# Strided values in two pieces, late constants, bf16 maxima and one tile width: a change to an attention and mixture-of-experts kernel

## The chip, the cores and the metric

The kernel runs on one NeuronCore of a Trainium2 chip. It has five engines with an instruction stream each: TensorE (matrix products into the accumulator memory PSUM), VectorE, ScalarE, GpSimd and SyncE, which here only starts transfers. Sixteen DMA engines move data between HBM and the on-chip memory SBUF; transfers are started by SyncE (most), ScalarE (five constants at the start) and GpSimd. The metric is the device time of one execution in microseconds, the median of several runs.

## What is computed

A batch of 8 sequences of 576 tokens passes 8 attention heads of width 64. The first four heads are local (a query sees itself and the 31 keys before it), the last four strided (a query sees the keys before it at distances that are multiples of 32). Then 4,608 tokens of width 512 are assigned to 8 experts, each with a capacity of 576 tokens, in the order of the gate's logits, and every expert is a two-layer network.

```python
scores = scale * np.matmul(q, k.transpose(0, 1, 3, 2))
rel = pos[:, None] - pos[None, :]
mask_local = (rel >= 0) & (rel < stride)
mask_strided = (rel >= 0) & (pos[None, :] % stride == pos[:, None] % stride)
...
attn = np.exp(scores - np.max(scores, axis=-1, keepdims=True))
attn = attn / (np.sum(attn, axis=-1, keepdims=True) + 1e-09)
x = np.matmul(attn, v)          # then [tokens, heads * 64]
...
logits = x @ w_gate             # greedy, largest logit first, capacity N // E
h = np.maximum(x[mask] @ w1[e], 0.0)
out[mask] = h @ w2[e]
```

## The kernel before, in words

Attention is worked off in 16 units (class `Unit`, list `todo`): for each of the 8 batches first the four strided heads, then the four local ones. A unit has two halves `p`, each a pair of heads, so there are 32 half-units, and the loop over `i` (the steps) runs from -1 to 31. It is an order written out by hand: in step `i` the scores of half-unit `i + 1` are finished (`close_scores`), its maxima taken, half-unit `i` is multiplied with the values (`mix`) and normalised (`norm`), the scores of half-unit `i + 2` are begun (`open_scores`), and then the maxima of `i + 1` are subtracted and the exponential is taken (`shift`). Dictionaries of small jobs (`fills`, `drips`, `mids`, `late`) are worked off at given steps: the f16 copy of the attention output (`finish`), its store to a scratch tensor in HBM (`store`), the transposed reload (`turn`), gate logits, scales.

The strided heads are stored sorted by residue, so that a strided head becomes a block-diagonal one: 32 residues of 18 positions. A half of the sequence (288 positions) is cut into 6 groups: five of 54 positions (3 residues, `SQ`) and a last one of 18 (`SLAST`, 288 - 5 x 54). The two sequence halves sit on partitions 0 to 63 and 64 to 127. In `dots` (L341 to 350) a group's scores are four matmuls with the keys as the stationary operand; in `mix` (L382 to 394) a group's output is, for each head of the pair, two matmuls with the exponentials `pr` as the stationary operand and the values `vn` (4 heads by 65 columns, the 65th a one for the sum) as the moving one. For the last group both use 18 columns of the array (`u.wide`, L277), for the others 54. The local heads use groups of 32 queries and 64 keys.

The maxima (`max_main` L352, `max_t` L356): VectorE reduces the scores by blocks of 32 with a transpose, TensorE spreads the result, VectorE reduces it again into `mr` (L362), and L364 to L367 make of it a pair of bf16 numbers (rounded value and remainder) and a diagonal matrix `dd`, with which TensorE subtracts the maxima from the scores in PSUM (L372). ScalarE takes the exponential from there (L376).

Loads are issued by SyncE in the program's order (`load` L305, `load_v` L315): the values of a unit as two transfers, one for each sequence half (54 partitions for a strided unit, 32 for a local one), then keys and queries as one each. Unit `k` is loaded at the start of step `2 (k - 3)`, units 0 to 3 ahead of the loop. The values live in two buffers for each kind, so the load waits until the unit two batches earlier has been mixed. SyncE also issues the reload of transposed outputs (L446), about half of the strided stores (L436; GpSimd issues the rest) and the local stores (L440, L441). Its waits hold up whatever stands behind them. Transfers of SyncE and ScalarE use a ring of eight semaphores: each issue waits until the transfer eight before it has landed.

Ahead of the loop, behind the loads of units 0 to 3, `late_constants` (L164, called in L572) loads seven tables that routing uses: `desc_h`, `fold`, `small`, `tri`, `pick`, `iota`, `val`. The first of them to be read is `desc8h`, in jobs from step 24 on (`PEAKS`).

After attention come routing (searches for the threshold of each expert) and the expert networks, in which weights are loaded, split into f16 parts and multiplied. The change does not touch that code.

Of the kernel before, what the change touches and what calls it, by code (L numbers as in the profile page):

```python
# [8 lines left out]
F32 = mybir.dt.float32  # L9
# [3 lines left out]
AF = mybir.ActivationFunctionType  # L13
OP = mybir.AluOpType
# [4 lines left out]
B, H, S, D = 8, 8, 576, 64  # L19
# [4 lines left out]
HS = S // 2  # L24
LT, LQ, LK = 9, 32, 64
ST, SR = 6, 3
SQ = SR * NA
SLAST = HS - (ST - 1) * SQ
NB = S // 32
BANK = 512  # L30
OPEN_S, OPEN_L = 1, 3
MAX_FIRST = True
WARM = {(-2, 0): 11, (-1, 0): 3, (-1, 2): 3, (31, 0): 2}
B_LATE, L_AT, G5, GW_AT = 5, 8, 6, 4
# [98 lines left out]
def band_stride_attention_then_capacity_moe(ctx, tc, qt, kl, ks, nl, ns, wg, w1, w2, cst, out, dbg=None):  # L133
# [30 lines left out]
    def late_constants():  # L164
        for t, name in ((desc8h, "desc_h"), (fold, "fold"), (small, "small"), (tri, "tri"), (pick, "pick"), (iota, "iota")):
            split_of = {"iota": NC, "pick": 2 * NT}.get(name)
            nc.sync.dma_start(t, cst[name].rearrange("q (s c) -> q s c", c=split_of) if split_of else cst[name])
        nc.sync.dma_start(val[:, :2], cst["val"].rearrange("q (a c) -> q a c", a=2))
# [51 lines left out]
    with tc.tile_pool(name="ld", bufs=2) as ld, \  # L220
# [12 lines left out]
        nc.scalar.activation(warm_e, ones_f[:, :1], AF.Exp)  # L233
        po_all = ps_o.tile([128, 2, BANK], F32, name="po")
        nc.vector.memset(po_all, 0.0)
        for g in "sl":
            for i in range(2):
                t = ld.tile([128, 32], F32, name=f"mx_{g}{i}", bufs=1)
                nc.gpsimd.memset(t, 0.0)
                mxb[g, i] = t  # L240
                t = ld.tile([128, ST if g == "s" else LT, 4, VW], F32, name=f"v_{g}{i}", bufs=1)
                nc.gpsimd.memset(t[:, 0] if g == "l" else t, 0.0)
                vbuf[g, i] = t
# [21 lines left out]
        class Unit:  # L265
# [39 lines left out]
            def load(u, parts=(slice(0, 2),), v=True):  # L305
                b, g = u.b, u.g
                if v:
                    u.load_v()
                u.kt = ld.tile([128, 2, u.nk], F32, name="k" + g)
                u.q = ld.tile([128, 2, S], F32, name="q" + g)  # L310
                for p in parts:
                    nc.sync.dma_start(u.kt[:, p], (ks if u.strided else kl)[b, :, p])
                    nc.sync.dma_start(u.q[:, p], qt[b, :, u.p0 + p.start:u.p0 + p.stop])

            def load_v(u):  # L315
                u.vn = vbuf[u.g, u.b % 2]
                for f in range(2):
                    r = slice(64 * f, 64 * f + SQ) if u.strided else slice(64 * f + 32, 64 * f + 64)
                    nc.sync.dma_start(u.vn[r], (ns if u.strided else nl)[u.b, f])

            def copy_v(u, k):
                vn, n = u.vn, LT // 3
# [18 lines left out]
            def dots(u, p, ts_):  # L341
                for t in ts_:
                    n = u.wide(t)
                    o = u.nq * t
                    for f, h in ((0, 0), (1, 1), (0, 1), (1, 0)):
                        c = HS * f + SQ * t if u.strided else LQ * (2 * t + f)
                        m = n if u.strided else LK
                        r = slice(64 * h, 64 * h + 64)
                        nc.tensor.matmul(u.sp[p][64 * f:64 * f + m, h, o:o + n], u.kt[r, p, c:c + m], u.q[r, p, c:c + n],
                                         start=False, stop=False, skip_group_check=True)  # L350

            def max_main(u, p):  # L352
# [3 lines left out]
            def max_t(u, p):  # L356
                pm = u.sp[p][:, 1, HS:HS + 64]
                for k in range(4):
                    nc.tensor.matmul(pm[32 * k:32 * k + 32], mxb[u.g, p], ident[:, 64 * (k % 2):64 * (k % 2) + 64],
                                     start=False, stop=False, skip_group_check=True)  # L360
                mr = wk.tile([128, 32], F32, name="mr")
                nc.vector.tensor_reduce(mr, pm.rearrange("r (g c) -> r c g", c=32), axis=AX.X, op=OP.max)  # L362
                mh = wk.tile([128, 32], BF16, name="mh")
                nc.vector.tensor_copy(mh, mr)  # L364
                nc.vector.tensor_tensor(mh[64:], mr[64:], mh[64:], op=OP.subtract)
                u.dd = wk.tile([128, NB, 32], BF16, name="dd")
                nc.vector.tensor_tensor(u.dd, mh[:, None, :].to_broadcast([128, NB, 32]), bm, op=OP.mult)  # L367

            def shift(u, p):
                df = u.dd.rearrange("r n c -> r (n c)")  # L370
                for h in range(2):
                    nc.tensor.matmul(u.sp[p][:, h, :HS], sel, df[:, HS * h:HS * h + HS], start=False, stop=True,  # L372
                                     skip_group_check=True)
                pr = wk.tile([128, S], F32, name="pr")
                u.pr[p] = pr
                nc.scalar.activation(pr.rearrange("k (h n) -> k h n", h=2), u.sp[p][:, :, :HS], AF.Exp, scale=0.125)  # L376

            def slots(u, ts_):
                a, b = (0, u.nt) if ts_ is None else (ts_[0], ts_[-1] + 1)
# [2 lines left out]
            def mix(u, p, h, ts_=None, po=None):  # L382
                j0, j1 = u.slots(ts_)
                n = j1 - j0
                po = po_all[:, h, :n * VW] if po is None else po[:, h * n * VW:(h + 1) * n * VW]
                po = po.rearrange("q (t d) -> q t d", d=VW)
                pr = u.pr[p]
                for t in range(u.nt) if ts_ is None else ts_:
                    n, o = u.wide(t), u.place(t, h)
                    for f in range(2):  # L390
                        j, r = (t, 64 * f) if u.strided else (t // 2, 64 * (t % 2) + 32 * f)
                        k = slice(64 * f, 64 * f + 64)
                        nc.tensor.matmul(po[r:r + n, j - j0], pr[k, o:o + n], u.vn[k, t, 2 * p + h],  # L393
                                         start=(j == j0), stop=(j == j1 - 1), skip_group_check=True)

            def norm(u, p, ts_=None, po=None):
# [172 lines left out]
            u.load_v()  # L569
        for u in todo[2:4]:  # L570
            u.load(v=False)
        late_constants()  # L572
        last = 2 * nu - 1
        edge = (B - 2) * S // TP

# [29 lines left out]
        for i in range(-1, 2 * nu):  # L605
            u, n, m = pair(i), pair(i + 1), pair(i + 2)
            if i > 0 and i % 2 == 0 and i // 2 + 3 < nu:
                todo[i // 2 + 3].load()
            if n:
                close_scores(n)  # L610
            warm(i, 0)
            for f in drips.get(i, []):
                f()
            if m or i in mids:
                a = room(m) if m else ps_a.tile([128, 2, 512], F32, name="spa")
            if i in mids or i in mids2 or i in mids3:
                b = ps_b.tile([128, 512], F32, name="spb")
            if u:
                if u[1] == 0:
                    u[0].begin()  # L620
                if i < last:
                    u[0].mix(u[1], 0)
            if i < last:
                for f in mids.get(i, []):
                    f(a, b)
            if i == last:
                gate_scale(B - 1)
                warm(i, 1)
                pt = ps_a.tile([128, 2, 512], F32, name="spa")
                pt = pt[:, 0], pt[:, 1]  # L630
                p1 = ps_b.tile([128, 512], F32, name="spb")
                for ts_, p_ in zip(parts, (None, p1)):
                    for h in range(2):
                        u[0].mix(u[1], h, ts_, p_)
                    u[0].norm(u[1], ts_, p_)
                break
            if n and MAX_FIRST:
                n[0].max_t(n[1])
            if u:
                u[0].mix(u[1], 1)  # L640
            if n and not MAX_FIRST:
                n[0].max_t(n[1])
            if i == last - 1:
                gates(B - 2, ps_a.tile([128, 2, 512], F32, name="spa"))
            warm(i, 1)
            if m:
                open_scores(m)
            warm(i, 2)
            if u:
                u[0].norm(u[1])  # L650
            if i in mids2:
                mids2[i].total_v(b)
            if i == 1:
                todo[1].scale_v()
            for f in mids3.get(i, []):
                f(a, b)
            if i == -1:
                todo[0].square_v()
            if n:
                n[0].shift(n[1])  # L660
            warm(i, 3)
            if i in (-1, 0):
                todo[1].square_v(i + 1)
            if i == 0:
                nc.scalar.activation(jkw, wg_sb, AF.Square, accum_out=sqw)
            for f in late.get(i, []) + fills.get(i, []):
                f()
# [659 lines left out]
```

## Time and profile before

| what | value |
|---|---|
| median of 3 runs (lowest, highest) | 732.16 us (729.22, 738.2) |
| the profiled execution | 732.86 us, of it the span of its instructions 731.1 us |
| attention, about | 0 to 236 us |
| routing and experts | 236 to 731 us |
| TensorE clock granted, mean of the span | 0.871 |
| moved by the DMA engines | 111.23 MB in 106,873 packets |

The page of a profile lists busy times of engines, the DMA queues, groups of equal instructions and their waits. Further views answer from the same trace: a table of busy times by stretch (columns: length, then busy us and, in brackets, instructions of PE, PEld, DVE, ACT and POOL, then granted TensorE clock, mean busy share of the 16 DMA engines and GB/s), a timeline (start, length, engine, line, operation, output<-inputs, shape, count and, in square brackets, idle time before it with what ended it), waits (engine, line, what it waited for: us in total, times, longest) and the DMA queues of a stretch (packets, MB, share of the engines' time). PE is the matmul side of TensorE and PEld its weight loads; DVE is VectorE, ACT ScalarE, POOL GpSimd, SPq SyncE's queue. `L349` is line 349 of the kernel. "issue" as a releaser says that the profile shows nothing that the engine waited for.

### The profile page before, as it was taken

Reading aid. Unit: us, or ns where it says so; the run is one execution under the profiler, and the core shown is the slowest. Engines: PE = TensorE matmul, PEld = TensorE weight load, DVE = VectorE, ACT = ScalarE, POOL = GpSimd, SP = SyncE. Lnnn points to the kernel's source line nnn. Section 1 sums busy time; section 2 is a strip of 40 time slices with the busy share of each in tenths; the row PEclk is TensorE's granted clock in tenths of the full one; section 3 lists DMA queues with packets and bytes.
Section 4 is the critical chain, followed back from the end, with each engine's and each line's share of the span. In section 5 each row is a group of like instructions: output and inputs, shape, how many; then the busy total and the mean of one; then the engine's idle time right before and its main releaser. Section 6 shows DMA issues by size and latency. Waiting matters only on the chain.

```text
span 731.1 us, 19141 instructions
## 1 busy us (share of the span) xinstructions
PE 622.4 (85%) x8043; PEld 410.6 (56%) x8043; DVE 456.3 (62%) x1368; ACT 320.2 (44%) x497; POOL 154.1 (21%) x152
## 2 busy tenths in 40 slices
PE   6878886875889348999999997998998997999993
PEld 3656664654667326645845743754754753665741
DVE  3686666754787777887677674776766763652200
ACT  3444334435252024757166273356347345853210
POOL 2043223133133011032032032015005014212011
PEclk8575657878696557999999998999999999999998
DMA  9989999799764145076076087067068069561010
GB/s 217 247 244 251 215 237 202 210 238 173 212 133 97 36 159 160 1 281 146 1 281 144 1 288 139 1 229 183 16 218 207 1 222 254 211 114 51 1 37 29
DMA packets 106873, 111.23 MB, mean 152 GB/s; under 512 B 75644, under 2 KB 83414, under 8 KB 106275
## 3 DMA queue, kind: packets, MB, share of 16 engines
q1 hardware_dynamic: 98707, 88.46, 47.4%
q0 software_dynamic: 7360, 21.15, 9.5%
q8 instruction: 63, 1.03, 0.6%
q10 hardware_dynamic: 720, 0.39, 0.2%
q14 instruction: 23, 0.19, 0.1%
HBM read 73.60 MB, written 18.87 MB: 126 GB/s over the span
## 4 chain that ended last, share of the span: by engine, by line
PE 21%; DMA 14%; issue 13%; DVE 8%; SPq 4%; ACT 2%; POOL 2%; POOLq 0%; ACTq 0%; DVEq 0%
PE ph L1155 16%; DMA w<-in_w_dram 8%; DMA xg<-x_scr,idx 3%; SPq L1071 3%; PE ph L1203 3%; DMA xt<-xg 2%; DVE w2l L1017 2%; SPq L983 1%; POOL out_dram L1214 1%; ACT jk L998 1%; DVE hl L1163 1%; POOL xg L1068 1%; DVE cm L774 1%; ACT yl L1210 0%; DVE y L1211 0%
## 5 line engine op out<-in xcount | busy, mean ns | idle before, releaser
L1155 PE MATMUL ph<-xt,w1h 128*128 128x288 f16 (+2 forms) x1024 | 179.8, 291 | 13.0 <-DMA xt<-xg 9.4
L1155 PEld LDWEIGHTS <-w1h 128*128 128x128 f16 x1024 | 98.6, 99 | 44.2 <-issue 9.2
L1214 POOL DMA_INDIRECT out_dram<-y,idx x40 | 43.6, 1091 | 342.2 <-ACT y L1213 314.4
L1155 PE MATMUL ph<-xt,w1l 128*128 128x288 f16 (+2 forms) x512 | 113.9, 292 | 0.0
L998 ACT ACTIVATE jk<-w 128x1024 f16<-128x1024 f32 x64 | 67.5, 1054 | 75.1 <-DMA w<-in_w_dram 73.2
L1203 PE MATMUL ph<-w2h,hh 128*128 128x512 f16 x256 | 97.0, 379 | 0.0
L1203 PE MATMUL ph<-w2h,hl 128*128 128x512 f16 x256 | 97.0, 379 | 0.0
L1203 PE MATMUL ph<-w2l,hh 128*128 128x512 f16 x256 | 97.0, 379 | 0.0
L1162 ACT ACTIVATE hh<-ph 128x576 f16<-128x576 f32 (+2 forms) x72 | 42.9, 596 | 120.3 <-PE ph L1155 117.6
L1203 PEld LDWEIGHTS <-hh 128*128 128x128 f16 x512 | 48.4, 98 | 59.6 <-issue 9.7
L1163 DVE SCALAR_TENSOR_TENSOR hl<-ph,hh 128x576 f16<-128x576 f32 (+2 forms) x72 | 49.5, 688 | 42.2 <-ACT hh L1162 41.9
L376 ACT ACTIVATE pr<-spa 128x576 f32<-128x576 f32 x32 | 20.8, 650 | 110.3 <-PE spa L372 92.9
L1155 PEld LDWEIGHTS <-w1l 128*128 128x128 f16 x512 | 50.6, 100 | 13.8 <-issue 0.8
L424 POOL TENSOR_TENSOR xos<-xs,xos 118x768 f16<-118x768 f32 x16 | 26.7, 1672 | 122.8 <-ACT xos L423 122.8
L1068 POOL DMA_INDIRECT xg<-x_scr,idx x40 | 41.6, 1039 | 49.0 <-issue 34.7
L1017 DVE SCALAR_TENSOR_TENSOR w1l<-w,w_sw,w1h 128x512 f16<-128x512 f32 x64 | 45.8, 747 | 9.1 <-ACT w1h L1016 3.9
L1017 DVE SCALAR_TENSOR_TENSOR w2l<-w,w_sw,w2h 128x512 f16<-128x512 f32 x64 | 45.8, 745 | 7.9 <-ACT w2h L1016 7.8
L393 PE MATMUL po<-v_s,pr 64*54 64x65 f32 (+1 forms) x768 | 42.7, 268 | 7.2 <-issue 4.7
L1213 ACT ACTIVATE y<-ph,so 128x512 f32<-128x512 f32 x32 | 21.9, 683 | 57.4 <-PE ph L1203 37.8
L1016 ACT ACTIVATE w1h<-w,w_sw 128x512 f16<-128x512 f32 x64 | 41.7, 709 | 3.2 <-DVE ss_e L203 1.8
L1016 ACT ACTIVATE w2h<-w,w_sw 128x512 f16<-128x512 f32 x64 | 41.1, 710 | 3.7 <-DVE w_sw L208 3.6
L1203 PEld LDWEIGHTS <-hl 128*128 128x128 f16 x256 | 25.0, 98 | 29.4 <-issue 3.6
(613 smaller groups left out, 972.6 us busy)
## 6 DMA issues: line engine op xcount, KB each, us to landing
w<-in_w_dram SPq DMA_DIRECT2D x64, 512.0 KB
v_s<-in_ns_dram SPq DMA_DIRECT2D x16, 329.1 KB
kl<-in_kl_dram SPq DMA_DIRECT2D x8, 608.0 KB
v_l<-in_nl_dram SPq DMA_DIRECT2D x16, 292.5 KB
ql<-in_qt_dram SPq DMA_DIRECT2D x8, 576.0 KB
x_scr<-xol SPq DMA_DIRECT2D x8, 512.0 KB
ks<-in_ks_dram SPq DMA_DIRECT2D x7, 576.0 KB
qs<-in_qt_dram SPq DMA_DIRECT2D x7, 576.0 KB
```

Of the source, the lines that this page charges most:

```text
L393: nc.tensor.matmul(po[r:r + n, j - j0], pr[k, o:o + n], u.vn[k, t, 2 * p + h], start=(j == j0), stop=(j == j1 - 1), skip_group_check=True)
L424: eng.tensor_tensor(u.xo[:nr, :, 1, c], xf, u.xo[:nr, :, 0, c], op=OP.subtract)
L998: nc.scalar.activation(jk, wf[:, c * n4:(c + 1) * n4].rearrange("p c f -> p (c f)"), AF.Square, scale=1.41422, accum_out=sq[:, c:c + 1])
L1016: nc.scalar.activation(hi[:, c, f], wf[:, c, f], AF.Copy, scale=s_)
L1017: nc.vector.scalar_tensor_tensor(lo[:, c, f], wf[:, c, f], s_, hi[:, c, f], op0=OP.mult, op1=OP.subtract)
L1068: nc.gpsimd.indirect_dma_start(out=xg[:n], out_offset=None, in_=x_rows, in_offset=bass.IndirectOffsetOnAxis(ap=idx[:n, t:t + 1], axis=0))
L1071: nc.sync.dma_start_transpose(xt[:, :, t * 128:t * 128 + n], xg[:n])
L1155: nc.tensor.matmul(tile_[:, j, :w], wt[:, d, f * 128:(f + 1) * 128], xt[:, d // 2, xx, d % 2, c], start=(k == 0), stop=(k == 3 * DC - 1))
L1162: nc.scalar.activation(hv, src, AF.Relu)
L1163: nc.vector.scalar_tensor_tensor(lv, src, 0.0, hv, op0=OP.max, op1=OP.subtract)
L1203: nc.tensor.matmul(py, a[:, f, ts_], w[:, f], start=(k == 0), stop=(k == len(todo) - 1))
L1214: st = nc.gpsimd.indirect_dma_start(out=out_rows, out_offset=bass.IndirectOffsetOnAxis(ap=idx[:n, t:t + 1], axis=0), in_=y[:n], in_offset= ...
```

## The change

- The values of a strided unit are loaded as four transfers in place of two: for each sequence half 48 rows and then 6.
- `late_constants` is called in step 13 of the loop, ahead of that step's other work and after the loads of step 12, in place of ahead of the loop.
- `mh`, the maxima rounded to bf16, is written by a VectorE operation with two operands (the maximum of `mr` with itself) in place of a copy.
- The last strided group uses 54 columns of the array like the others, in `dots` and in `mix`. For that the stationary operands are read past their end: strided keys and exponentials move into fixed buffers (`ktb`, `prb`) with 36 further columns, which GpSimd fills at the start with zeros and ones. The further rows of the scores are masked, the further rows of the output are not stored. In the first key half the read reaches into the second key half's columns. The number of matmuls is the same.

```diff
@@ constants, set-up
+CONST_AT = 13
...
+        ktb = [ld.tile([128, 2 * S + SQ - SLAST], F32, name=f"ks{i}", bufs=1) for i in range(2)]
+        prb = [wk.tile([128, S + SQ - SLAST], F32, name=f"pr{i}", bufs=1) for i in range(2)]
+        for i in range(2):
+            nc.gpsimd.memset(ktb[i][:, 2 * S:], 0.0)
+            nc.gpsimd.memset(prb[i][:, S:], 1.0)
@@ load
-                u.kt = ld.tile([128, 2, u.nk], F32, name="k" + g)
+                u.kt = ktb[b % 2] if u.strided else ld.tile([128, 2 * u.nk], F32, name="kl")
...
-                    nc.sync.dma_start(u.kt[:, p], (ks if u.strided else kl)[b, :, p])
+                    nc.sync.dma_start(u.kt[:, p.start * u.nk:p.stop * u.nk].rearrange("q (p n) -> q p n", n=u.nk),
+                                      (ks if u.strided else kl)[b, :, p])
@@ load_v
                 for f in range(2):
-                    r = slice(64 * f, 64 * f + SQ) if u.strided else slice(64 * f + 32, 64 * f + 64)
-                    nc.sync.dma_start(u.vn[r], (ns if u.strided else nl)[u.b, f])
+                    for i, n in ((0, 48), (48, SQ - 48)) if u.strided else ((0, 32),):
+                        r = 64 * f + (i if u.strided else 32)
+                        nc.sync.dma_start(u.vn[r:r + n], (ns if u.strided else nl)[u.b, f, i:i + n])
@@ dots
-                        m = n if u.strided else LK
+                        m = SQ if u.strided else LK
...
-                        nc.tensor.matmul(u.sp[p][64 * f:64 * f + m, h, o:o + n], u.kt[r, p, c:c + m], u.q[r, p, c:c + n],
+                        nc.tensor.matmul(u.sp[p][64 * f:64 * f + m, h, o:o + n], u.kt[r, p * u.nk + c:p * u.nk + c + m], u.q[r, p, c:c + n],
@@ max_t
-                nc.vector.tensor_copy(mh, mr)
+                nc.vector.tensor_tensor(mh, mr, mr, op=OP.max)
@@ shift
-                pr = wk.tile([128, S], F32, name="pr")
-                u.pr[p] = pr
+                pr = u.pr[p] = prb[p]
...
@@ mix
-                    n, o = u.wide(t), u.place(t, h)
+                    o = u.place(t, h)
...
-                        nc.tensor.matmul(po[r:r + n, j - j0], pr[k, o:o + n], u.vn[k, t, 2 * p + h],
+                        nc.tensor.matmul(po[r:r + u.nq, j - j0], pr[k, o:o + u.nq], u.vn[k, t, 2 * p + h],
@@ order of the work
             u.load(v=False)
-        late_constants()
...
                 todo[i // 2 + 3].load()
+            if i == CONST_AT:
+                late_constants()
```

More of the change, by code (lines that the diff above doesn't have):

```diff
@@ L373, in shift @@
                                      skip_group_check=True)
-                pr = wk.tile([128, S], F32, name="pr")
-                u.pr[p] = pr
-                nc.scalar.activation(pr.rearrange("k (h n) -> k h n", h=2), u.sp[p][:, :, :HS], AF.Exp, scale=0.125)
+                pr = u.pr[p] = prb[p]
+                nc.scalar.activation(pr[:, :S].rearrange("k (h n) -> k h n", h=2), u.sp[p][:, :, :HS], AF.Exp, scale=0.125)
             def slots(u, ts_):
```

## The prediction

> **What bounds the kernel now.** I read the page first (slices, queues), then the table by stretches of time, the waits, the timeline of the longest gap, SyncE's timeline and the DMA view around that gap.
>
> ```profile
> PE 622.4 (85%) x8043; PEld 410.6 (56%) x8043; DVE 456.3 (62%) x1368; ACT 320.2 (44%) x497; POOL 154.1 (21%) x152
> ...
> q8 instruction: 63, 1.03, 0.6%
> ...
> 0.00:236.00 236.00, 186.31 (x4453) 134.53 (x4453) 155.19 (x419) 98.32 (x125) 66.97 (x69) 0.75 0.87 205
> ```
>
> The change touches attention alone, 0 to 236 us, where the DMA engines are 87% busy (second number from the right) and TensorE was granted 0.75 of its clock. Routing and experts start when the last logits exist, so what attention gains should reach the end one to one.
>
> ```profile
> SPq L319 <- PE po L393: 23.1, 7, 5.2
> ...
> 124.82 1.17 PE L349 MATMUL spa<-qs,ks 64*54 64x54 f32 x36 [5.70 <-issue]
> 183.97 0.26 PE L349 MATMUL spa<-qs,ks 64*18 64x18 f32 x6 [6.41 <-issue]
> ...
> 97.02:124.82 27.80, 19.99 (x510) 14.88 (x509) 17.95 (x46) 13.10 (x18) 9.30 (x8) 0.75 0.96 225
> ...
> q1 hardware_dynamic: 1208, 1.78, 105.4%
> ...
> q8 instruction: 1, 0.02, 5.4%
> ```
>
> TensorE's long gaps are put down to "issue": no semaphore that the profile knows ended them. From the end of the gap at 97.02 (row further below) to that at 124.82 lie 510 + 509 matmuls and weight loads, 1,024 with a few instructions of the sequencer. Queue q8 says why such a round number: 1.03 MB over 2 x 8043 instructions is 64 B each, so each of its 63 packets of 16 KB holds 256, and four packets 1,024. TensorE waits for its own instructions. The last two rows are the DMA view of 114.4 to 122.2 us (no q8 packet among 1,208 of q1) and of 122.2 to 123.4 (one q8 packet); TensorE resumes at 124.82. So that fetch went through only when a burst of loads had passed. Here is the burst on SyncE:
>
> ```profile
> 84.39 0.72 SPq L319 DMA_DIRECT2D v_s<-in_ns_dram  x2
> ...
> 86.11 8.66 SPq L446 DMA_TRANSPOSE xtl<-x_scr  x1
> ...
> 99.72 0.80 SPq L319 DMA_DIRECT2D v_l<-in_nl_dram  x2
> ...
> 101.70 6.58 SPq L446 DMA_TRANSPOSE xts<-x_scr  x1
> ...
> 111.67 1.18 SPq L319 DMA_DIRECT2D v_s<-in_ns_dram  x2
> 113.83 8.98 SPq L446 DMA_TRANSPOSE xtl<-x_scr  x1
> ...
> 113.00:114.60 1.60, 0.85 (x38) 0.61 (x37) 1.48 (x5) 0.36 (x1) 0.00 (x0) 1.00 0.51 168
> 118.50:119.50 1.00, 0.62 (x5) 0.29 (x4) 0.88 (x4) 0.34 (x1) 1.00 (x1) 1.00 0.91 304
> ...
> v_s<-in_ns_dram SPq DMA_DIRECT2D x16, 329.1 KB
> kl<-in_kl_dram SPq DMA_DIRECT2D x8, 608.0 KB
> v_l<-in_nl_dram SPq DMA_DIRECT2D x16, 292.5 KB
> ql<-in_qt_dram SPq DMA_DIRECT2D x8, 576.0 KB
> ks<-in_ks_dram SPq DMA_DIRECT2D x7, 576.0 KB
> ```
>
> A transpose's issue ends when the loads before it are through. The strided burst (values twice 329.1 KB, keys and queries 576 each, 1,810 KB) takes 94.77 - 84.39 = 10.4 us and 122.81 - 111.67 = 11.1; the local burst (1,769 KB) 108.28 - 99.72 = 8.6. The stretch 113.0 to 114.6, when only the 54-row values move, has 0.51 of the DMA engines busy at 168 GB/s; with keys and queries, 0.91 at 304. So 54 rows use about 9 of 16 engines. The loop is thus: SyncE waits for a mix (23.1 us in 7 waits) to free the value buffer, the burst runs, TensorE waits for instructions behind it.
>
> **The change part by part.** The sum is made against the profiled execution, 732.9 us (0.7 above the median of 732.16).
>
> *48 and 6 rows.* Per engine the two 54-row loads put 12 rows on nine engines. 48 divides by 16 as the local 32 rows do; with 3 + 1 rows twice, the fullest engine has 8. A burst as even as the local one would take 8.6 x 1,810 / 1,769 = 8.8 us: 1.6 to 2.3 us less than the two shown. I take 1.9. Bounds: at worst all 6 rows go through one engine, which then has 6 + 12 rows, half as much again as now, and the burst is longer by about as much (+1.9); at best 2.3. Each strided burst is followed by a fetch wait, which can shrink by no more than itself:
>
> ```profile
> 47.05 0.42 PE L349 MATMUL spa<-ql,kl 64*64 64x32 f32 x12 [0.92 <-issue]
> 68.84 1.07 PE L393 MATMUL po<-v_l,pr 64*32 64x65 f32 x27 [1.99 <-issue]
> ...
> 97.02 1.08 PE L393 MATMUL po<-v_l,pr 64*32 64x65 f32 x30 [1.35 <-issue]
> ...
> 153.90 0.43 PE L359 MATMUL spa<-ident,mx_s 128*32 128x64 f32 x4 [3.84 <-issue]
> ...
> 21.80 0.86 PE L349 MATMUL spa<-ql,kl 64*64 64x32 f32 x24 [1.23 <-DMA ql<-in_qt_dram]
> 31.64 1.50 PE L349 MATMUL spa<-ql,kl 64*64 64x32 f32 x45 [2.08 <-issue]
> ```
>
> 0.9 + 1.9 + 1.35 + 1.9 x 3 (97 to 184 us: 5.7, 3.8 and 6.4 long) = 9.9 us. The two strided loads at the start shorten the waits at 21.8 and 31.6 by 1.2 + 1.9 = 3.1. The 16 added issues cost SyncE 0.4 us each (0.72 for two at 84.39), in front of the keys: nothing, because the engines are still on the values then; without that cover 2 x 0.4 us a burst.
>
> *Constants at step 13.*
>
> ```profile
> 24.02 0.33 SPq L167 DMA_DIRECT2D desc8h<-in_c_desc_h_dram  x1
> ...
> 34.55 0.33 SPq L168 DMA_DIRECT2D val<-in_c_val_dram  x1
> 36.07 0.69 SPq L319 DMA_DIRECT2D v_s<-in_ns_dram  x2
> ...
> 108.97 0.51 SPq L441 DMA_DIRECT2D x_scr<-xol  x1
> ...
> iota<-in_c_iota_dram SPq DMA_DIRECT2D x1, 576.0 KB
> ```
>
> Seven issues of 0.33 us go from 24 to 35 us to SyncE's gap 109.5 to 111.7, ahead of the load at 111.67; behind them wait that load, its transpose and the stores. Issuing fits the gap (2.3 of 2.2 us). Of their data iota's 576 KB take 1.9 us at 304 GB/s, the six smaller ones by my estimate half as much again, 2.8 together, of which SyncE's gap hides some 0.5: that burst is later by 0 to 2.8 us, and as the DMA engines are nearly always busy I take 2.3. At the start the load at 36.07 may move ahead by up to 10 us; nothing waited for its data, so I book 0, but see the rivals.
>
> *Maxima.*
>
> ```profile
> 46.35 3.65 DVE L364 CAST mh<-mr 128x32 bf16<-128x32 f32 x1
> ...
> 47.20 2.75 POOL L424 TENSOR_TENSOR xol<-xl,xol 128x640 f16<-128x640 f32 x2
> 50.77 0.64 PE L372 MATMUL spa<-dd,sel 128*128 128x288 bf16 x2 [2.99 <-DVE dd L367]
> ...
> L364 DVE CAST mh<-mr x32: 181/181/3654, 9.6 to 228.7; 128x32 bf16<-128x32 f32 x32
> L365 DVE TENSOR_TENSOR mh<-mr,mh x32: 189/189/190, 9.8 to 228.9; 64x32 bf16<-64x32 f32 x32
> ```
>
> One CAST held on until GpSimd was done at 49.95, and TensorE stood 2.99 us for it. The two-operand operation beside it never exceeded 190 ns. At 0.19 us the matrix is ready before TensorE comes: 3.0 us gained. Bounds: 31 x 8 ns lost if it blocks just as the CAST did, 3.5 gained.
>
> [...]
>
> *No 32-column tiles.*
>
> ```profile
> L393 PE MATMUL po<-v_s,pr 64*54 64x65 f32 x640 | 33.9, 269 | 7.2 <-issue 4.7 <-DVE xs L411 1.6 <-ACT pr L376 0.8
> L393 PE MATMUL po<-v_s,pr 64*18 64x65 f32 x128 | 11.0, 259 | 0.0
> ```
>
> Same moving size, but 86 ns of TensorE per narrow matmul against 53: 128 x 33 ns = 4.2 us. The scores' narrow ones (128) I take as no gain. The wider weight loads lie in the 54-column rate. What is saved before a fetch wait is swallowed by it; I take 3.0, ends 0 and 4.2. Four memsets on GpSimd at the start and the read past a key half cost nothing: the value loads wait for SyncE's ring, the keys land before.
>
> **Sum**: 9.9 + 3.1 - 2.3 + 3.0 + 3.0 = 16.7; 732.9 - 16.7 = 716.
>
> **The rivals.** *The clock follows.* Shorter waits may also let TensorE keep more of its clock. At 0.80 in place of 0.75 the 186 busy us of attention would be 175, and another 12 us go: 704. For it speaks that the granted clock is 0.75 here and 1.00 right before the longest gap (row of 118.5). Against: the DMA engines are at 0.87 already and then become the bound.
>
> *New collisions.* Without the constants the load of 36.07 follows todo[3]'s at once, and the fetches of 31.6 and 36.1 us, which waited little, come to lie behind a burst as that of 114.4 did: two waits of up to 5.7 us eat 11: 727. For it: with the constants gone nothing on SyncE holds that load but the ring of earlier loads and the mix of step 1. Against: the fetches behind bursts that began at 36 and 57 us cost 0.9 and 2.0 us, not 5.7.
>
> *The fetch lies on one of the seven free engines.* Then even values lengthen its queue, from keys and queries alone to 6 more rows. Rows of 6 KB at 168 / 9 = 19 GB/s take 0.33 us: +2 us at six bursts, and no gain of 9.9 and 1.9: 732.9 + 12 - 1.2 - 6.0 + 2.3 = 740. Against: seven engines without values would have been through with keys and queries some 2 to 3 us before 122, and the fetch did not go then.
>
> *Slower: each added transfer costs a slot.* The seven constants took 34.9 - 24.0 = 10.9 us, 1.55 each, for little data. If 16 more value transfers took that each: +24.8 with only 6.0 - 2.3 gained: 754. It decides from 16.7 / 16 = 1.0 us a transfer. Against: two value loads are issued within 0.72 us at 84.39, and the constants' slots fall in a stretch where the ring was full of the first loads. [...]
>
> **How the numbers follow.** Forecast 0.50 (own range 709 to 723), clock 0.18, collisions 0.18, free engine 0.08, slot 0.06. 2% of 732.16 is 14.6 us, about what a measurement of this kernel can tell: faster below 717.5, which is 0.30 of the forecast's 0.50 and the clock's 0.18: 0.48; slower above 746.8: the slot, 0.06; same 0.46. The range from 704 to 730 leaves out the last two cases, 0.14.
>
> **What would show it.** In the profile after: with only values moving, the DMA share near 0.9; strided bursts of 9 us; the waits after them about 2 us shorter, except the one near 125; no gap of 3 us at step 5; L364 at 0.19 us throughout. The forecast is wrong if fetch waits turn up after 30 to 45 us, if bursts stay at 10 us, or if the waits shrink and TensorE then waits for data.

## The result and the profile after

The changed kernel took 726.85 us (median of 20 runs, 717.12 to 734.09), the kernel before in the same comparison 734.86 us (20 runs): a ratio of 0.986, 95% interval 0.983 to 0.990. The ratio leaves out runs more than 1.5% above the fastest of their kernel, so it is not the quotient of the two medians (0.989). It is faster by 1.4%, which is 10.1 us of 734.86 (7.6 to 12.6). The forecast of 716.0 against 732.16 was 0.978.

The profiled execution of the changed kernel took 722.58 us, its span 720.6. First the page, which is hardly different as a whole; then, from the table by stretches, attention up to its last exponential, of the kernel before and of the changed one (columns as above: length, busy us and instructions of PE, PEld, DVE, ACT and POOL, granted clock, DMA share, GB/s):

```profile
PE 612.3 (85%) x8040; PEld 409.5 (57%) x8043; DVE 456.9 (63%) x1368; ACT 319.9 (44%) x497; POOL 153.9 (21%) x156
...
q8 instruction: 63, 1.03, 0.6%
```

```profile
0.00:230.60 230.60, 181.95 (x4361) 131.11 (x4361) 151.75 (x406) 96.41 (x121) 65.17 (x65) 0.74 0.88 208
```

```profile
0.00:222.50 222.50, 174.01 (x4359) 130.95 (x4361) 153.76 (x408) 96.35 (x122) 66.35 (x69) 0.77 0.92 216
```

Attention ends 8.1 us earlier, and TensorE is busy for 7.9 us less, so its idle time stayed as it was (48.7 and 48.5 us). The bytes are the same, 208 x 230.6 = 216 x 222.5 = 48 MB, so the shorter time is at once a rate that is 4% higher.

The forecast looked for the gain in the waits for instructions. Here they are in the changed kernel, from TensorE's timeline, with the wait for `dd` at step 5 among them:

```profile
35.93 0.40 PE L346 MATMUL spa<-mask_s,ident_b 128*128 128x288 bf16 x1 [3.12 <-issue]
50.69 0.64 PE L380 MATMUL spa<-dd,sel 128*128 128x288 bf16 x2 [4.28 <-DVE dd L375]
68.56 0.95 PE L400 MATMUL po<-v_l,pr 64*32 64x65 f32 x28 [4.10 <-issue]
82.30 0.34 PE L468 MATMUL spa<-xts,wgh 128*32 128x288 f16 x1 [2.67 <-issue]
95.10 1.09 PE L400 MATMUL po<-v_l,pr 64*32 64x65 f32 x32 [2.96 <-issue]
123.69 0.44 PE L357 MATMUL spa<-qs,ks 64*54 64x54 f32 x6 [2.51 <-issue]
138.61 0.27 PE L400 MATMUL po<-v_s,pr 64*54 64x65 f32 x1 [4.29 <-issue]
175.71 0.56 PE L357 MATMUL spa<-qs,ks 64*54 64x54 f32 x12 [3.53 <-issue]
```

With one of 0.89 us at 163.4 these sum to 24.1 us (over 0.8 us each, from 20 us on, without `dd`), against 26.5 before. The waits near 125 and 184 shrank from 5.7 and 6.4 to 2.5 and 3.5, but those of 35.9 and 138.6 are new or larger. SyncE's timeline shows the bursts:

```profile
25.85 1.48 SPq L327 DMA_DIRECT2D v_s<-in_ns_dram  x4
...
84.36 1.54 SPq L327 DMA_DIRECT2D v_s<-in_ns_dram  x4
...
87.09 7.81 SPq L453 DMA_TRANSPOSE xtl<-x_scr  x1
...
107.87 0.98 SPq L168 DMA_DIRECT2D desc8h<-in_c_desc_h_dram  x1
...
111.85 1.53 SPq L327 DMA_DIRECT2D v_s<-in_ns_dram  x4
...
116.42 7.21 SPq L453 DMA_TRANSPOSE xtl<-x_scr  x1
```

The load that stood at 36.07 now stands at 25.85. Measured as in the forecast, from the first value load to the end of the transpose's issue (in the kernel before 5.4 to 9.3 us long behind the bursts from 57 us on, 2.1 to 3.4 with no load ahead, from 187 us on), the two bursts take 94.90 - 84.36 = 10.5 us and 123.63 - 111.85 = 11.8: no shorter than the 10.4 and 11.1 before. The five strided bursts from 50 us on last 10.9 us on average, against 10.7. The next row is a stretch in which only values move, to be held against the one with 0.51 and 168 GB/s in the prediction:

```profile
166.80:168.60 1.80, 1.46 (x76) 1.12 (x68) 1.74 (x3) 1.78 (x2) 0.00 (x0) 1.00 0.96 215
```

All engines work, as forecast, but each moves less: 215 / (0.96 x 16) = 14.0 GB/s against 168 / (0.51 x 16) = 20.6. A burst's two value loads, 658 KB, take 3.1 us at 215 GB/s in place of 3.9.

### The profile page after: what moved, and what is told of

It is laid out like the page before. It is cut to its first block, busy times and chain, and to the rows that moved or that the text cites. A ratio compares the mean times of both kernels' runs of the same rounds, so it can differ in the third digit from the quotient of the medians.

```text
span 720.6 us, 19175 instructions
## 1 busy us (share of the span) xinstructions
PE 612.3 (85%) x8040; PEld 409.5 (57%) x8043; DVE 456.9 (63%) x1368; ACT 319.9 (44%) x497; POOL 153.9 (21%) x156
## 4 chain that ended last, share of the span: by engine, by line
PE 22%; issue 17%; DMA 12%; DVE 6%; SPq 4%; POOL 3%; ACT 2%; POOLq 0%; ACTq 0%; DVEq 0%
PE ph L1163 16%; DMA w<-in_w_dram 5%; DMA xg<-x_scr,idx 4%; SPq L1079 3%; PE ph L1211 3%; DMA xt<-xg 2%; DVE w2l L1025 2%; POOL xg L1076 1%; POOL out_dram L1222 1%; ACT jk L1006 1%; SPq L991 1%; PE ph L1205 1%; DVE hl L1171 1%; DVE cm L828 0%; PE ph L1064 0%
## 5 line engine op out<-in xcount | busy, mean ns | idle before, releaser
L1163 PEld LDWEIGHTS <-w1h 128*128 128x128 f16 x1024 | 98.6, 99 | 46.9 <-issue 11.1
L400 PE MATMUL po<-v_s,pr 64*54 64x65 f32 x768 | 38.4, 262 | 9.6 <-issue 7.9
L1221 ACT ACTIVATE y<-ph,so 128x512 f32<-128x512 f32 x32 | 21.8, 682 | 54.5 <-PE ph L1211 33.9
```

The source lines that it names most:

```text
L400: nc.tensor.matmul(po[r:r + u.nq, j - j0], pr[k, o:o + u.nq], u.vn[k, t, 2 * p + h], start=(j == j0), stop=(j == j1 - 1), skip_group_check ...
L1163: nc.tensor.matmul(tile_[:, j, :w], wt[:, d, f * 128:(f + 1) * 128], xt[:, d // 2, xx, d % 2, c], start=(k == 0), stop=(k == 3 * DC - 1))
L1221: nc.scalar.activation(y, py, AF.Copy, scale=so[:, t:t + 1])
```

## The experiments

Ratios are to the kernel before, of the same comparison, with 95% intervals. One profile is one execution of runs that spread by 13 us (before) and 17 us (changed), so verdicts go by ratios, and single waits serve only to show a mechanism.

**Each part alone** (on the kernel before), and the maxima read from PSUM.

The values:

```diff
-                    r = slice(64 * f, 64 * f + SQ) if u.strided else slice(64 * f + 32, 64 * f + 64)
-                    nc.sync.dma_start(u.vn[r], (ns if u.strided else nl)[u.b, f])
+                    for i, n in ((0, 48), (48, SQ - 48)) if u.strided else ((0, 32),):
+                        r = 64 * f + (i if u.strided else 32)
+                        nc.sync.dma_start(u.vn[r:r + n], (ns if u.strided else nl)[u.b, f, i:i + n])
```

> The kernel before with the strided values in 48 and 6 rows alone. Theory A (the gain of the whole change, ratio 0.986, is spread over the parts, and the even spread is worth less than I booked because a row takes longer when all engines carry one): ratio 0.990 to 0.996, 3 to 7 us. Rival B (the values are the whole gain): 0.984 to 0.988. In both the share of busy DMA engines while only values move rises from about one half to above 0.9; by A the strided bursts stay above 10 us.

Measured: 723.18 us against 735.95, 0.979 (0.974 to 0.983): 15.6 us (12.3 to 18.9). The split alone gives at least what the whole change gives (the two intervals just touch at 0.983), and more than either theory allowed. Its five strided bursts from 50 us on last 11.1 us on average: that part of theory A held.

The last group with 54 columns in `dots` and `mix`, with `ktb` and `prb` (one line of that part of the change):

```diff
-                        m = n if u.strided else LK
+                        m = SQ if u.strided else LK
```

> The kernel before with the 54-column last group alone (fixed key and exponential buffers with it). Theory A: the narrow matmuls' 4.2 us of TensorE shrink to the rate of the others and about half arrives: ratio 0.994 to 0.998. Rival B: nothing arrives, since instruction fetches behind the loads set the pace: 0.998 to 1.002.

Measured: 0.996 (0.992 to 1.001): 2.6 us, from a gain of 6.2 to a loss of 1.0. Its row for attention, and below it the one group of the mix in the changed kernel that takes the place of the two of before (33.9 + 11.0 us):

```profile
0.00:232.10 232.10, 171.80 (x4360) 128.98 (x4361) 154.00 (x408) 96.29 (x122) 65.42 (x69) 0.77 0.92 207
```

```profile
L400 PE MATMUL po<-v_s,pr 64*54 64x65 f32 x768 | 38.4, 262 | 9.6 <-issue 7.9
```

TensorE is busy 10 us less than before, yet attention ends no earlier: the waits for instructions of over 0.8 us, from 20 us on, sum to 33.1 in place of 26.5. In this profile the work that went ahead of such waits was waited for instead.

The constants:

```diff
-        late_constants()
...
+            if i == CONST_AT:
+                late_constants()
```

> The kernel before with the constants at step 13 alone. Theory A: the load of todo[4] starts some 10 us earlier and a fetch near 35 us then waits behind it, the burst near 112 us is late by about 2 us: ratio 0.998 to 1.004. Rival C (the constants at the start were what held up attention): 0.990 to 0.995.

Measured: 1.005 (1.001 to 1.010): a loss of 4.0 us (0.8 to 7.1), just past theory A.

The maxima in PSUM, on the changed kernel, so that L372 and L373 have at most one SBUF input:

```diff
-                mr = wk.tile([128, 32], F32, name="mr")
+                mr = u.sp[p][:, 1, HS + 64:HS + 96]
...
-                nc.vector.tensor_tensor(mh, mr, mr, op=OP.max)
+                nc.vector.tensor_reduce(mh, pm.rearrange("r (g c) -> r c g", c=32), axis=AX.X, op=OP.max)
```

> The changed kernel with mr kept in PSUM and mh taken by a second reduction from PSUM, so that neither of the two operations on the maxima has two SBUF inputs. Theory A (the 3.67 us operation at step 5 waits for GpSimd because both its inputs are in SBUF): no operation on the maxima above 0.5 us, TensorE's wait of 4.28 us at 50.7 us falls below 1, and the lead over the kernel before that was zero at step 5 is 2 us or more there; ratio 0.979 to 0.984. Rival D (the operation waits for something that GpSimd's descriptors or another engine hold, whatever its operands): the wait stays above 3 us and the ratio at 0.986.

Measured: 0.995 (0.991 to 0.999). First the changed kernel around step 5, VectorE, then GpSimd, then all 32 of L372 (shortest, median and longest in ns); then the same place of this experiment:

```profile
46.26 3.67 DVE L372 TENSOR_TENSOR mh<-mr 128x32 bf16<-128x32 f32 x1
...
44.88 2.21 POOL L443 DMA_DIRECT2D x_scr<-xos  x3 [0.32 <-POOL xos L431]
47.11 2.75 POOL L431 TENSOR_TENSOR xol<-xl,xol 128x640 f16<-128x640 f32 x2
...
L372 DVE TENSOR_TENSOR mh<-mr x32: 191/193/3668, 9.6 to 219.8; 128x32 bf16<-128x32 f32 x32
```

```profile
L372 DVE TENSOR_REDUCE mh<-spa x32: 224/225/226, 8.4 to 219.9; 128x32 bf16<-128x64 f32 x32
...
47.86 3.57 DVE L375 TENSOR_TENSOR dd<-mh,bm 128x576 bf16<-128x576 bf16 x1
...
48.35 2.75 POOL L431 TENSOR_TENSOR xol<-xl,xol 128x640 f16<-128x640 f32 x2
...
51.48 0.40 PE L380 MATMUL spa<-dd,sel 128*128 128x288 bf16 x1 [4.03 <-DVE dd L375]
```

With both inputs in SBUF the two-operand operation took 3.67 us at step 5 and ended when GpSimd's two had (49.93 and 49.86), as the CAST, which has one input, had (3.65 us). With the input in PSUM it took 0.23 us at most, and the next operation with two SBUF inputs, L375, took 3.57, against 0.46 in the changed kernel. TensorE's wait for `dd` is the same, 4.03 us against 4.28. Why this kernel is 0.8% slower than the changed one in the runs, its span (721.4 us) doesn't show; that stays open.

**Is it the sixteen engines, or the cutting?** The kernel before with 27 and 27 rows; the lines show it against the first experiment:

```diff
-                    for i, n in ((0, 48), (48, SQ - 48)) if u.strided else ((0, 32),):
+                    for i, n in ((0, 27), (27, 27)) if u.strided else ((0, 32),):
```

> The kernel before with the strided values as 27 and 27 rows in place of 48 and 6: as many transfers as in the change, rows not divisible by 16. Theory (the gain of 48 + 6 comes from using all sixteen engines, and 27 rows lie on nine): packets of 6,240 B stay near 415 ns, the stretch with values alone stays near half of the DMA share, ratio 0.995 to 1.005. Rival (any cut in two lets small things through between the pieces, or shortens them): ratio 0.985 or less. Rival (an added transfer costs): over 1.005.

Measured: 0.993 (0.989 to 0.997). With values alone in flight, first here, then in the first experiment (48 and 6 rows alone):

```profile
111.50:113.40 1.90, 1.82 (x86) 1.38 (x84) 1.07 (x2) 1.52 (x2) 0.00 (x0) 1.00 0.46 163
...
166.30:168.30 2.00, 2.00 (x88) 1.44 (x86) 0.60 (x2) 1.19 (x2) 0.00 (x0) 0.86 0.94 209
```

Half of the engines, as before, at 163 / (0.46 x 16) = 22 GB/s each, which is 0.28 us for a row of 6,240 B (in the trace of the kernel before the 864 rows of 6,240 B took 418 ns on average, those of the stretch of 113.0 us 301). The cut itself brings 0.7%, a little more than the theory allowed; the rest of the 2.1% came only with the rows that use all engines. The 16 added transfers cost nothing that the runs show.

**The place of the constants.** The changed kernel with the constants ahead of the loop again:

```diff
+        late_constants()
...
-            if i == CONST_AT:
-                late_constants()
```

> The changed kernel with the constants loaded ahead of the loop again. Theory (parts add: values alone 0.979, constants alone 1.005, maxima and tiles about nothing): ratio 0.975 to 0.983, and the load of todo[4] issues near 36 us again, so the wait of 3.1 us for instructions at 35.9 goes. Rival (with the values split, the late constants cost nothing): the ratio stays 0.986. The wait for dd near 50 stays 3 to 4.5 us in both.

Measured: 713.75 us against 737.13, 0.973 (0.966 to 0.979): the fastest kernel that does the whole work, and clear of the changed kernel's interval. The load of `todo[4]` issues at 31.3 us, and the wait of 3.1 at 35.9 is gone.

`desc_h` alone at step 13, the other six at step 27, 200 us in (`late_constants` takes a flag that says which):

```diff
-            if i == CONST_AT:
-                late_constants()
+            if i in (CONST_AT, 27):
+                late_constants(i == CONST_AT)
```

> The changed kernel with desc_h alone at step 13 and the other six constants at step 27, 200 us in. Theory (the constants cost their 1 MB of transfers wherever the DMA engines are full, and their early place holds todo[4]'s load back): the burst near 112 is 2 us earlier, the wait at 123.7 shrinks, the 2 us come back near 200: ratio 0.982 to 0.988. Rival (the late steps have bytes to spare): 0.980 or less.

Measured: 0.980 (0.971 to 0.988): the value is the rival's, and the interval covers both theories.

The constants loaded twice, ahead of the loop and at step 13:

```diff
+        late_constants()
         last = 2 * nu - 1
```

> The changed kernel with the constants loaded both ahead of the loop and at step 13: the load of todo[4] is held to about 31 us as without the move, and the 1 MB lies ahead of the later burst as in the change. Theory A (the late place costs through todo[4]'s earlier load and the fetch behind it): the wait near 36 of 3.1 us goes, ratio within 0.005 of 0.973. Theory B (it costs through the bytes ahead of the burst of 112 us): that burst begins about 2 us late, ratio 0.978 to 0.987.

Measured: 0.989 (0.983 to 0.995): theory B, at a little more than its 0.978 to 0.987. The load of `todo[4]` is held to 32.7 us and the wait near 36 is gone, but nothing is gained by that. The four kernels form a square: with all of the tables ahead of the burst at 112 us 0.986 and 0.989, with `desc_h` alone or none 0.980 and 0.973; with `todo[4]` early 0.986 and 0.980, held 0.989 and 0.973. What is loaded at step 13 matters, the early load hardly; 0.980 and 0.986 have intervals that overlap, so the square is carried by its other corners. The table by stretches shows where the early place has its room, first of the changed kernel, then of the one with the constants ahead:

```profile
0.00:40.00 40.00, 29.81 (x574) 20.13 (x579) 20.83 (x61) 15.97 (x19) 3.94 (x16) 0.72 0.89 242
...
80.00:120.00 40.00, 31.62 (x863) 24.41 (x865) 26.82 (x70) 19.25 (x23) 13.11 (x12) 0.79 0.96 234
```

```profile
0.00:40.00 40.00, 30.47 (x667) 20.49 (x669) 23.78 (x70) 19.27 (x25) 6.08 (x18) 0.83 0.95 264
...
80.00:120.00 40.00, 29.69 (x853) 22.81 (x846) 26.64 (x72) 19.55 (x23) 12.72 (x12) 0.83 0.99 236
...
0.00:214.80 214.80, 168.98 (x4360) 126.36 (x4361) 154.66 (x408) 96.47 (x121) 65.64 (x69) 0.80 0.90 224
```

The first 40 us had room: with the constants there 264 GB/s instead of 242, 0.9 MB more in 40 us, about what the seven tables are (856 KB by their issues), at no loss of TensorE's work (667 matmuls against 574). From 80 to 120 us the engines are at 0.96 with the tables and at 0.99 without: no room there.

How the late place costs 1.3% these profiles do not show. Here is the start of the thirteenth exponential in the changed kernel, with the constants ahead, and with the constants loaded twice:

```profile
99.80 0.65 ACT L383 ACTIVATE pr<-spa 128x576 f32<-128x576 f32 x1 [5.02 <-PE spa L380]
...
89.91 0.65 ACT L382 ACTIVATE pr<-spa 128x576 f32<-128x576 f32 x1 [0.75 <-PE spa L379]
...
96.98 0.65 ACT L383 ACTIVATE pr<-spa 128x576 f32<-128x576 f32 x1 [5.02 <-PE spa L380]
```

The kernel with the constants ahead leads the changed one by 9.9 us here, before the late tables are issued (107.87), and by 7.7 us at the last exponential. The second and the third kernel are the same program up to step 13, and yet lie 7.1 us apart: a lead of that size in one profile can be chance. The bytes explain at most a part of some 10 us: 0.9 MB at 234 GB/s are 3.8 us. The seven issues also keep SyncE from 107.87 to 111.75 us, in front of the load of 111.85; no run tells these from the bytes.

**Does a fetch wait for the burst ahead of it?** Keys and queries one step after the values:

```diff
-                todo[i // 2 + 3].load()
+                todo[i // 2 + 3].load_v()
+            if i > 1 and i % 2 == 1 and i // 2 + 3 < nu:
+                todo[i // 2 + 3].load(v=False)
```

> The changed kernel with the keys and queries of a unit loaded one step after its values, so that a strided burst of 1,810 KB falls into 658 and 1,152 KB. Theory (a fetch of instructions waits for the whole burst in front of it): the waits for instructions of over 0.8 us, 24.1 us in all in the changed kernel, sum to 17 or less, none over 3.5 us, ratio 0.98 or less. Rival (the DMA engines are full in attention, the waits are only where the lack of bytes shows): the sum stays within 21 to 27 or turns into waits for data, ratio 0.983 to 0.99. Keys that come too late would show as waits for ks, qs, kl or ql.

Measured: 0.984 (0.978 to 0.990), waits for instructions 24.0 us in all, one of them 5.45, against 24.1 in the changed kernel: the rival. Cutting the burst in two did not free the fetches.

Fewer bytes:

```diff
+                if u.strided and b > 1:
+                    u.kt, u.q = ktb[b % 2], todo[2 * (b - 2)].q
+                    return
```

> The changed kernel without the loads of strided keys and queries from the third batch on (the tiles of two batches before are used, so the output is another one); 6 x 1,152 KB less, the strided bursts are the values alone. Theory (a fetch of instructions is held up by the burst in front of it): from 70 us on the waits for instructions behind strided bursts (82.3: 2.7, 95.1: 3.0, 123.7: 2.5, 163.4: 0.9, 175.7: 3.5, near 12.6 us together with 0 to 2 more) fall under 4 us in all, and attention ends 8 us earlier or more, ratio 0.975 or less. Rival (fetches are slow whatever lies in front): the waits stay at 10 us or more, the time falls by less than 4 us. Rival (bytes alone bound attention): DMA share stays at 0.9 and the end comes 6.9 MB / 0.21 MB per us = 33 us earlier.

Measured: 710.12 us against 733.89, 0.971 (0.963 to 0.978). TensorE's waits for instructions of 1 us or more from 66 us on, and attention:

```profile
112.50 0.31 PE L360 MATMUL spa<-qs,ks 64*54 64x54 f32 x5 [2.66 <-issue]
124.75 0.30 PE L349 MATMUL spa<-mask_l,ident_b 128*128 128x288 bf16 x1 [1.97 <-issue]
130.26 0.89 PE L403 MATMUL po<-v_l,pr 64*32 64x65 f32 x28 [2.02 <-issue]
149.25 0.28 PE L471 MATMUL spa<-xtl,wgh 128*32 128x288 f16 x1 [2.21 <-issue]
```

```profile
0.00:201.30 201.30, 157.87 (x4359) 118.25 (x4361) 150.52 (x406) 96.82 (x122) 66.66 (x69) 0.88 0.90 203
```

Two of the four lie behind strided bursts (value loads at 103.2 and 124.0 us), 4.7 us where the theory wanted under 4 and the changed kernel had about 12.6. All waits for instructions over 0.8 us sum to 12.9 us, against 24.1. Attention ends 21 us earlier in this profile: more than the 8 that the fetch theory asked for at least, less than the 33 of bytes alone. The DMA share stays at 0.90, as the theory of bytes said; 16 us of the 21 appear as shorter busy time of the same matmuls, at a granted clock of 0.88.

**GpSimd at step 5.** The first finished unit's copy on VectorE, on the changed kernel:

```diff
-                at(2 * j + p if j else 2, lambda u=u, p=p: u.finish(p, nc.gpsimd))
+                at(2 * j + p if j else 2, lambda u=u, p=p: u.finish(p, nc.vector if u is todo[1] else nc.gpsimd))
```

> The changed kernel with the f16 copy of the first finished unit's outputs (L424, at step 5 on GpSimd) on VectorE. Theory (L372 has two SBUF inputs and waits until GpSimd's two tensor operations are through): L372's longest near 46 us falls from 3.67 us to 0.2, the wait of TensorE for dd of 4.28 at 50.7 goes. Of it 1 to 2.5 us reach the end: ratio 0.982 to 0.985. Rival (the wait only uncovers the next fetch): the dd wait goes, but a wait for instructions nearby grows by as much: ratio 0.986. Rival (another operation of GpSimd than this one holds VectorE): the 3.67 us stay.

Measured: 0.984 (0.980 to 0.988), not to be told from the changed kernel. The wait for `dd` at step 5 is gone, and VectorE, which now does the copy, is late with something else. Below that line is L372 in the same profile, and GpSimd issuing transfers meanwhile:

```profile
44.54 0.33 PE L367 MATMUL spa<-ident,mx_s 128*32 128x64 f32 x4 [4.66 <-DVE mx_s L361]
...
46.45 0.19 DVE L372 TENSOR_TENSOR mh<-mr 128x32 bf16<-128x32 f32 x1
...
45.61 2.21 POOL L443 DMA_DIRECT2D x_scr<-xos  x3 [0.32 <-POOL xos L431]
```

The two halves of that copy apart, on the kernel with the constants ahead:

```diff
-                at(2 * j + p if j else 2, lambda ...
+                at((2 * j + p + (p if j == 1 else 0)) if j else 2, lambda ...
```

> The changed kernel with the constants ahead of the loop again, and the second half of todo[1]'s f16 copy (L424) one step later on GpSimd, so that its two tensor operations no longer follow each other. Theory (VectorE's operation with two SBUF inputs waits until the GpSimd operations in a row are through): its longest falls from 3.67 to about 2 us, the wait for dd from 4.3 to about 2.5; ratio 0.968 to 0.973. Rival (the wait only uncovers another): 0.973 to 0.977.

Measured: 0.980 (0.974 to 0.986), no gain over 0.973. The mechanism is as supposed: GpSimd's first half alone meets no operation with two SBUF inputs, the second does (L371 1.02 us against 0.19, ended 54.21; GpSimd 54.15), and L372 behind L371 waits too, until GpSimd's next operation is through (1.56 us against 0.19, ended 55.80; GpSimd 55.75).

```profile
45.25 1.41 POOL L430 TENSOR_TENSOR xol<-xl,xol 128x640 f16<-128x640 f32 x1
52.54 1.61 POOL L430 TENSOR_TENSOR xol<-xl,xol 128x640 f16<-128x640 f32 x1 [5.87 <-ACT xol L429]
54.12 1.63 POOL L430 TENSOR_TENSOR xos<-xs,xos 118x768 f16<-118x768 f32 x1
...
48.27 0.19 DVE L371 TENSOR_TENSOR mh<-mr 128x32 bf16<-128x32 f32 x1
53.19 1.02 DVE L371 TENSOR_TENSOR mh<-mr 128x32 bf16<-128x32 f32 x1
54.24 1.56 DVE L372 TENSOR_TENSOR mh<-mr,mh 64x32 bf16<-64x32 f32 x1
...
56.34 0.41 PE L379 MATMUL spa<-dd,sel 128*128 128x288 bf16 x2 [2.26 <-DVE dd L374]
```

The wait for `dd` fell from 4.35 us to 2.26, and the end did not come earlier.

## Why the prediction was right in sign and too large in size

| term | forecast, us | measured, us |
|---|---|---|
| values as 48 and 6 rows | -13.0 | alone -15.6 (-18.9 to -12.3) |
| constants at step 13 | +2.3 | alone +4.0 (0.8 to 7.1); on top of the rest, 0.973 to 0.986, about 10 |
| maxima | -3.0 | not timed alone; its operation waits as long as the CAST, the wait for `dd` stays |
| last group 54 columns wide ("no 32-column tiles") | -3.0 | alone -2.6 (-6.2 to +1.0) |
| all | -16.7 | -10.1 (-12.6 to -7.6) |

*Values: the sum near by luck, the path not as worked out.* The step that failed is "A burst as even as the local one would take ... 8.8 us". It supposed that sixteen engines move rows at the pace of nine; the row of 166.8 us shows 14.0 GB/s per engine in place of 20.6, so a burst's values need 0.8 us less, not 1.9, and with the longer issues the bursts became no shorter (10.9 us against 10.7, and 11.1 with the split alone). Nor did the waits behind strided bursts shrink by 9.9 us: those of over 0.8 us from 20 us on fell by 4.5 in all with the split alone. What the runs show is that the rows on all engines bring the gain, and not the cut: 48 and 6 rows 0.979, 27 and 27 rows 0.993. How it becomes time stays open. Attention in the profile of the split alone:

```profile
0.00:223.10 223.10, 180.51 (x4361) 130.68 (x4361) 155.40 (x406) 96.30 (x122) 65.54 (x65) 0.76 0.93 215
```

It ends 7.5 us earlier than before, with the same bytes and TensorE idle for 42.6 us in place of 48.7. That is half of the 15.6 us that the runs show, and about what two profiles of one program differ by (7.1 us above). That the waits for instructions hang on the bytes is borne out (without a seventh of the bytes half of the waits go, 12.9 us left of 24.1, though the DMA share stays at 0.90); that they wait for the burst in front to pass is not, since a burst cut in two left the waits at 24.0 us.

*Constants: the mis-sized term.* It priced 2.8 us of transfers at 112 us and none of the room that they left unused in the first 40 us. Both the 2.3 and the 2.8 at the upper end of "0 to 2.8" are under what the runs show, if the kernel with the constants ahead is the measure (1.3% of 735 us); alone the loss is 0.5%, whose interval of 0.8 to 7.1 us leaves the 2.3 possible. How about 10 us come of it stays open, as said above.

*Maxima: wrong.* "The two-operand operation beside it never exceeded 190 ns" was true of an operation that ran only when the blocked one had been let go. In the changed kernel the operation did block, 3.67 us at step 5 with both inputs in SBUF; with the input in PSUM it took 0.23 us at most. It started ahead of GpSimd's two, at 46.26 against 47.11, and waited all the same. GpSimd was issuing transfers from 44.88 on, but issuing alone did not hold the operation: with the first unit's copy on VectorE, L372 ran at 46.45 in 0.19 us while GpSimd issued from 45.61 to 47.82. What held it from 46.26 to 47.11 is not settled; times on GpSimd are rough.

*Tiles: right in size* within a wide interval, and the rows show why little of it can arrive. No view shows a tile of 32 columns for that group: the profile before names it `64*18`, that after `64*54`.

*The rivals.* New collisions: the wait came where it was said, at 35.9 us, 3.1 long, but holding that load back did not pay (0.989 against 0.986). The clock: it rose from 0.74 to 0.77, not the 0.80 of that rival; with the constants ahead it is 0.80, and the time 713.75. The free engine and the slot are out: 48 and 6 rows gained, and 27 and 27 did not lose. The small size of a piece did not decide here: pieces of 37 KB (36.6 by their issue) came with 2.1% less time.

Of the signs that the forecast named, the DMA share near 0.9 with values alone came; bursts of 9 us, a step 5 without a gap and L364 (now L372) at 0.19 us throughout did not. The waits near 125 and 184 us shrank by 3, not by 2, and others took their place. Of the three signs by which it called itself wrong two came: a wait for instructions at 35.9 us, and bursts that stayed over 10 us.

So the time came out within its range of 704 to 730 by terms that missed both ways: the constants cost about 8 us more than booked, the maxima brought nothing that the runs show, and the split made up for a part of that by a path that was not the one worked out. By its own 2% line (faster below 717.5 of 732.16) the change is "same", to which it gave 0.46, and "faster" 0.48.

## What to carry to other kernels

Where transfers fill the DMA engines, ask of each how many engines its rows use and how full they are at that moment: here cutting an uneven transfer, even into a small piece, was worth 2.1%, and a table loaded "later" cost 1.3%, where the early stretch had room (242 GB/s, 264 with the tables in it) and the late one none (80 to 120 us: DMA share 0.96 with them, 0.99 without). A fast operation that always runs behind a blocked one says nothing about whether it would block itself; look at what the two have in common (here, input read from SBUF, 3.67 us; read from PSUM, the wait was gone from that operation, 0.23 us at most, and came at the next one that reads SBUF alone, 3.57 us). Test parts alone before keeping a bundle: here one part alone gave at least the gain of all, and leaving out another made the kernel a further 1.3% faster.

## What the runs showed of the hardware that was not expected

Most waits for instructions in the changed kernel were followed by a lower clock. The table by stretches before and after the wait that ended at 95.10 us:

```profile
90.00:92.10 2.10, 1.98 (x53) 1.48 (x52) 1.44 (x5) 0.94 (x2) 1.75 (x2) 1.00 0.97 329
95.10:98.10 3.00, 3.00 (x78) 2.23 (x78) 1.29 (x5) 0.00 (x0) 1.16 (x1) 0.50 1.05 295
98.10:101.00 2.90, 2.90 (x62) 2.13 (x62) 1.31 (x4) 1.20 (x2) 0.00 (x0) 0.50 0.84 226
```

The granted clock was 1.00 before a wait of 2.96 us and 0.50 for the 5.9 us after it. In the same profile it was 1.00 before and 0.50 to 0.53 in the 1.7 to 3.2 us after the waits of 2.51, 2.67, 3.53, 4.10 and 4.29 us, and 1.00 in the 2.6 us after the one of 0.89; before and after the one of 3.12 it was 0.50. In the kernel with fewer bytes 36 matmuls of L403 took 0.76 us after the wait of 1.97 us (at 126.67) and 1.30 us after that of 2.02 us (at 135.83). What length it takes, and whether length decides, is open. The same matmuls of attention took 174.01, 168.98 and 157.87 us of TensorE at a mean granted clock of 0.77, 0.80 and 0.88 in the rows above, and a sum of waits alone leaves that out.

Value rows of 6 KB spread over all sixteen engines moved at 14.0 GB/s an engine (row of 166.8 us), over half of them at 20.6 (row of 113.0 us before): doubling the engines gave 28% more bytes per us.
